# Moving two DMA destinations in SBUF from 128 bytes past a multiple of 256 to a multiple of 4096

## The chip, the cores and the metric

One core of one Trainium2 chip. The metric is the device time of one execution in microseconds (us). A comparison uses runs of both kernels taken in the same rounds on the same chip. Single runs are marked as such below.

Some terms. HBM is the memory outside the core, SBUF the core's own memory, used here in 128 partitions. In this kernel's trace TensorE runs the matrix multiplications, VectorE copies and reductions, ScalarE the activations. A packet is the trace's record of a piece of work on one of the 16 DMA engines: a load of 8 MB gives 128 packets of 64 KB, as many as there are partitions. By a descriptor the text means the order for one such piece, so it takes a packet for a descriptor. "PV" in the prediction is the multiplication of the probabilities with the values.

## The reference

Two attention layers decode one token each, and their outputs stand side by side. Layer A has 32 heads and reads all 32768 keys of each; layer B has 32 query heads on 8 key heads and reads the last 4096 keys. Everything is bfloat16.

```python
def _A_ref(x, k_cache, v_cache, wq, wo):            # H = 32, Sk = 32768, Dh = 128
    q = (x @ wq).reshape(B, Sq, H, Dh)...
    scores = einsum("bhqd,bhkd->bhqk", q, k_cache) * Dh ** -0.5
    o = einsum("bhqk,bhkd->bhqd", softmax(scores), v_cache)
    return o... @ wo
# B: the same over k_cache[:, :, Sk - 4096:, :] with 8 key heads
return concatenate([a, b], axis=-1)
```

Layer A's caches alone are 32 heads x 2 x 8 MB. Nothing is used twice, so the kernel is a stream from HBM with enough arithmetic beside it to keep up.

## The kernel before

All buffers are allocated one after another in each partition of SBUF. `kbuf` holds three parts of 32 KB a partition, `vbuf` two. A head of A needs two parts of each: 64 KB in each of 128 partitions, 8 MB. The head's keys are transposed on TensorE into `kt`, multiplied with the query, and the probabilities are multiplied with the values straight from `vbuf`.

```python
    def alloc(self):
        nc = self.nc
        sb = nc.alloc_sbuf_tensor
        self.kbuf = sb("kbuf", [128, 3 * HALF * DH], BF16)      # HALF = DH = 128
        self.vbuf = sb("vbuf", [128, 2 * HALF * DH], BF16)
        self.kt = [sb(f"kt{i}", [128, 1024], BF16) for i in range(NKT)]
        self.psb = sb("psb", [128, 512], BF16)
        # ... the small buffers ...

    def load(self, dst, src, sem, *deps):
        self.op("sp", lambda e: e.dma_start(dst, src).then_inc(sem, 16), *deps)

    # ...
    def kv_src(self, which, name, g):
        d = self.X[name]
        src = d[which][0, g * d["kvg"]:(g + 1) * d["kvg"], d["key0"]:d["key0"] + d["NKEYS"], :]
        return src.rearrange("s (p j) d -> p s (j d)", p=128)

    # ...
    def load_k(self, g, parts):
        w = HALF * DH
        src = self.kv_src("k", "A", g)[:, 0, :]
        lo = min(self.k_thirds(g))
        free = [self.free["k"][t] for t in self.k_thirds(g)]
        if parts == 1:                                          # heads 1 to 30
            self.load(self.kbuf[:, w * lo:w * lo + 2 * w], src, self.mark("k", 0), *free)
            sem = self.mark("k", 1)
            self.op("sp", lambda e: e.sem_inc(sem, 16), self.free["k"][0] if g == 1 else None)
        else:
            for i, t in enumerate(self.k_thirds(g)):
                self.load(self.kbuf[:, w * t:w * t + w], src[:, w * (t - lo):w * (t - lo) + w], self.mark("k", i), *free)

    def load_v(self, g):
        self.load(self.vbuf[:, :], self.kv_src("v", "A", g)[:, 0, :], self.mark("v", 0), *self.free["v"])
    # ... B's loads and the weights go into the same two buffers, in pieces of 3 to 32 KB a partition ...
```

The compiled program places `kbuf` at byte 16512 of each partition and `vbuf` at 114816; both are 128 past a multiple of 256.

## Time and profile before

| | before |
|---|---|
| time, median of 3 runs | 1327.09 us (1326.9 to 1327.21) |
| DMA queue 1, share of 16 engines' span | 99.7% |
| DMA rate, 100 to 1200 us | 433 to 434 GB/s |
| TensorE / VectorE busy | 73% / 57% |
| TensorE's wait for a head's keys | 157.2 us in 31 waits |

Two lines of the page's table of DMA queues. They give packets, MB, and the time that the packets took as a share of the span of 16 engines:

```profile
q1 hardware_dynamic: 13190, 570.44, 99.7%
...
HBM read 570.43 MB, written 0.00 MB: 431 GB/s over the span
```

Busy time by stretches of the span. After the stretch and its length come the engines' busy times, then the granted clock, the DMA share and GB/s as the last three numbers:

```profile
100.00:400.00 300.00, 217.86 (x2952) 151.61 (x2952) 163.90 (x289) 12.68 (x40) 0.00 (x0) 0.82 1.00 433
400.00:800.00 400.00, 300.08 (x4160) 211.24 (x4158) 234.82 (x411) 15.86 (x50) 0.00 (x0) 0.84 1.00 433
800.00:1200.00 400.00, 294.81 (x4057) 204.69 (x4054) 226.63 (x400) 17.44 (x55) 0.00 (x0) 0.84 1.00 434
```

A DMA share of 1.00 in all three, while no engine is busy more than 76% of a stretch, is what a kernel bound by its transfers looks like. The instruction groups say the same from the other side: count, busy time and mean of one, then the idle time before them and who ended it.

```profile
L563 DVE COPY kt<-psT 128x1024 bf16<-128x1024 bf16 x1056 | 654.8, 684 | 239.6 <-PE psT L559 237.6
L559 PE MATMUL psT<-ident,kbuf 128*128 128x128 bf16 x8448 | 578.2, 234 | 171.7 <-DMA kbuf<-in_A_k_cache_dram 157.2
...
L662 PE MATMUL psACC<-vbuf,ptsb 128*4 128x512 bf16 (+1 forms) x2112 | 186.2, 529 | 22.8 <-ACT ptsb L637 22.0
```

TensorE waits for a key landing once a head, 5 us on average. The DMA queue for its part waits for buffers to come free. From the list of waits, first the queue's own, then TensorE's (total us, times, longest):

```profile
SPq L326 <- PE psACC L662: 632.2, 32, 21.0
SPq L326 <- PE psS L582: 612.5, 35, 26.5
```

```profile
PE psT L559 <- DMA kbuf<-in_A_k_cache_dram: 157.2, 31, 10.0
...
PE psT L559 <- DMA kbuf<-in_B_k_cache_dram: 11.0, 2, 6.2
```

And from the table of DMA issues, where the last number is the median time from issue to landing in us:

```profile
vbuf<-in_A_v_cache_dram SPq DMA_DIRECT2D x32, 26.6
...
kbuf<-in_A_k_cache_dram SPq DMA_DIRECT2D x30, 27.8
```

The queue's long waits look alarming and are not: 8 MB at 434 GB/s take 19.3 us, and a load lands 26.6 to 27.8 us after its issue, so each is issued while the one ahead still runs and the engines do not run dry (DMA share 1.00 from 100 to 1200 us). A shorter transfer therefore shortens the kernel, by up to those 5 us a head. The unit to look at is the single packet. The trace has each packet of the queue with its size and duration; sorted by size, this is a count that the page does not print:

```
packets of queue 1, kernel before: bytes, count, median ns, the most frequent durations (ns, count)
65536 x7936  2422   2422 x2448, 2418 x1374, 2426 x1275, 2419 x1091, 2420 x673, 2421 x350, ...
16384 x256    615    615 x60,    611 x57,    619 x36, ...
 8192 x2176   312    309 x798,   314 x359,   312 x275, 321 x248, ...
 4096 x128    161    159 x52,    161 x16, ...
```

Between 16 and 64 KB the medians rise by 1807 ns for 49152 bytes, which is 1.176 ns for 32 bytes. The rest, about 12.6 ns at both sizes (10.8 at 8 KB, 10.4 at 4 KB), does not go with the bytes.

### The profile page before, as it was taken

The page shows a single profiled execution, that of the slowest core. Times are in us where ns is not written, and L with a number is a line of the kernel's source. Part 1 is how long each engine was busy: PE and PEld are TensorE (multiplying, and loading weights), DVE is VectorE, ACT ScalarE, POOL GpSimd, SP SyncE. Part 2 cuts the span into 40 slices and gives each one's busy share as a digit, 9 for nine tenths or more (in the row PEclk, how much of TensorE's full clock was granted, in tenths as well). Part 3 has the DMA queues.
Part 4 walks back from the last instruction along what each step waited for, and adds up shares of the span by engine and source line. Part 5 has one row for each costly group of instructions (what it writes and reads, how often), then busy time and mean ns, then how long its engine had stood idle before and what let it go on. Part 6 is the DMA issues. An engine that isn't in the chain of part 4 may idle for free. (4 is left out here: it accounts for less than half of the span.)

```text
span 1324.9 us, 28805 instructions
## 1 busy us (share of the span) xinstructions
PE 966.8 (73%) x13243; PEld 673.9 (51%) x13243; DVE 751.2 (57%) x1341; ACT 54.8 (4%) x167; POOL 2.6 (0%) x22
## 2 busy tenths in 40 slices
PE   4675778777677878767787876778786677868786
PEld 3453446555444655544465544446554445655453
DVE  3563556664555666455566645556664556665563
ACT  0000000000000000000000000000000000000000
POOL 0000000000000000000000000000000000000000
PEclk8886788887878888787888878788887879887898
DMA  9999999999999999999999999999999999999998
GB/s 403 430 434 430 441 429 427 441 435 427 436 433 437 427 437 435 427 439 431 427 441 433 435 429 433 437 427 439 434 427 439 431 431 437 431 437 429 433 437 350
DMA packets 13489, 570.60 MB, mean 431 GB/s; under 512 B 1827, under 2 KB 1830, under 8 KB 2214
## 3 DMA queue, kind: packets, MB, share of 16 engines
q1 hardware_dynamic: 13190, 570.44, 99.7%
q8 instruction: 8, 0.13, 0.0%
q10 hardware_dynamic: 288, 0.00, 0.0%
q14 instruction: 3, 0.02, 0.0%
HBM read 570.43 MB, written 0.00 MB: 431 GB/s over the span
## 5 line engine op out<-in xcount | busy, mean ns | idle before, releaser
L563 DVE COPY kt<-psT 128x1024 bf16<-128x1024 bf16 x1056 | 654.8, 684 | 239.6 <-PE psT L559 237.6
L559 PE MATMUL psT<-ident,kbuf 128*128 128x128 bf16 x8448 | 578.2, 234 | 171.7 <-DMA kbuf<-in_A_k_cache_dram 157.2
L559 PEld LDWEIGHTS psT<-ident,kbuf 128*128 128x128 bf16 x8448 | 538.5, 106 | 263.9 <-DMA kbuf<-in_A_k_cache_dram 165.3
L662 PE MATMUL psACC<-vbuf,ptsb 128*4 128x512 bf16 (+1 forms) x2112 | 186.2, 529 | 22.8 <-ACT ptsb L637 22.0
L582 PE MATMUL psS<-kt,qw 128*32 128x512 bf16 x2048 | 157.8, 385 | 15.0 <-DVE kt L563 15.0
L676 DVE TENSOR_SCALAR oc_A<-psACC,hot_A 128x128 f32<-128x128 f32 x32 | 11.2, 351 | 250.8 <-PE psG L689 250.8
L662 PEld LDWEIGHTS psACC<-vbuf,ptsb 128*4 128x4 bf16 (+1 forms) x2112 | 60.3, 111 | 139.1 <-issue 91.4
L610 ACT ACTIVATE psb<-psS,nb_A 128x512 bf16<-128x512 f32 x32 | 22.0, 687 | 1168.4 <-DVE nb_A L609 1168.4
L582 PEld LDWEIGHTS psS<-kt,qw 128*32 128x32 bf16 x2048 | 34.1, 95 | 57.6 <-DVE kt L563 30.7
L689 PE MATMUL psG<-oc_A,hw 128*32 128x128 f32 (+1 forms) x128 | 19.3, 227 | 52.3 <-DVE oc_A L678 52.3
L689 PEld LDWEIGHTS psG<-oc_A,hw 128*32 128x32 f32 x128 | 11.4, 109 | 62.4 <-DVE oc_A L678 55.1
L634 PE MATMUL psPT<-ident,psb 128*128 128x128 bf16 x136 | 18.1, 275 | 34.0 <-ACT psb L610 34.0
L678 DVE SCALAR_TENSOR_TENSOR oc_A<-psACC,hot_A,oc_A 128x128 f32<-128x128 f32 x96 | 33.7, 351 | 3.4
L599 DVE TENSOR_REDUCE tr_in<-psS 128x1 f32<-128x512 f32 x34 | 23.5, 692 | 17.3 <-PE psS L582 17.3
L634 PEld LDWEIGHTS psPT<-ident,psb 128*128 128x128 bf16 x136 | 10.2, 118 | 37.0 <-ACT psb L610 36.7
L603 PE MATMUL psACC<-rows,tr_in 128*1 128x64 f32 x64 | 8.7, 217 | 25.6 <-DVE tr_in L599 25.6
L637 ACT ACTIVATE ptsb<-psPT 128x512 bf16<-128x512 bf16 x34 | 20.3, 597 | 31.1 <-PE psPT L634 31.1
L603 PEld LDWEIGHTS psACC<-rows,tr_in 128*1 128x1 f32 x64 | 2.7, 81 | 35.3 <-DVE tr_in L599 35.3
L607 PE MATMUL psACC<-mr_A,nscale 1*128 1x1 f32 x64 | 12.1, 256 | 9.7 <-DVE mr_A L606 9.7
L607 PEld LDWEIGHTS psACC<-mr_A,nscale 1*128 1x128 f32 x64 | 9.4, 183 | 15.7 <-DVE mr_A L606 15.7
L609 DVE COPY nb_A<-psACC 128x1 f32<-128x1 f32 x32 | 5.0, 157 | 15.1 <-PE psACC L607 15.1
L606 DVE TENSOR_REDUCE mr_A<-psACC 1x1 f32<-1x64 f32 x32 | 6.8, 212 | 11.7 <-PE psACC L603 11.7
(81 smaller groups left out, 72.0 us busy)
## 6 DMA issues: line engine op xcount, KB each, us to landing
kbuf<-in_A_k_cache_dram SPq DMA_DIRECT2D x4, 4096.0 KB, 22.9
kbuf<-in_B_k_cache_dram SPq DMA_DIRECT2D x2, 4096.0 KB, 31.8
vbuf<-in_B_v_cache_dram SPq DMA_DIRECT2D x2, 4096.0 KB, 25.6
vbuf<-in_B_wq_dram SPq DMA_DIRECT2D x1, 4096.0 KB, 12.4
vbuf<-in_A_wq_dram SPq DMA_DIRECT2D x1, 4096.0 KB, 31.9
kbuf<-in_B_wo_dram SPq DMA_DIRECT2D x2, 2048.0 KB, 33.7
kbuf<-in_A_wo_dram SPq DMA_DIRECT2D x1, 1408.0 KB, 28.1
kbuf<-in_A_wo_dram SPq DMA_DIRECT2D x1, 1024.0 KB, 30.2
```

The source lines that it names most:

```text
L559: inst = e.transpose(T[:, 128 * k:128 * k + 128], src[:, DH * k:DH * k + DH], self.ident[:, :])
L563: self.copies.append(self.op("dve", lambda v: v.tensor_copy(KT[:, :], T[:, :]), o, to="pe"))
L582: inst = e.matmul(self.S[32 * c:32 * c + 32, :], lhsT=win, rhs=self.kt[(bb + c // 2) % NKT][:, 512 * (c % 2):512 * (c % 2) + 512], start=b ...
L599: o = dve(lambda v: v.reduce_max(tr["in"][:, 0:1], self.S[:, :], axis=AXX), self.sdone, self.k_pool, to="pe" if name == "A" else None)
L603: o = self.op("pe", lambda e: e.matmul(self.ACC[0:1, 0:64], lhsT=tr["in"][:, 0:1], rhs=self.rows64[:, :], start=True, stop=True, skip_grou ...
L607: o = self.op("pe", lambda e: e.matmul(self.ACC[:, 64:65], lhsT=self.nscale[:, :], rhs=t["mr"][0:1, :], start=True, stop=True, skip_group_ ...
L610: self.sread = self.op("act", lambda s: s.activation(out=self.psb[:, :], in_=self.S[:, :], func=ACTF.Exp, bias=t["nb"][:, k:k + 1], scale= ...
L634: inst = e.transpose(PT[:, 128 * jj:128 * jj + 128], self.psb[:, 128 * jj:128 * jj + 128], self.ident[:, :])
L637: self.ptread = self.op("act", lambda s: s.activation(out=self.ptsb[:, :], in_=PT[:, 0:512], func=ACTF.Copy), self.psread, to="pe")
L662: inst = e.matmul(acc[32 * c:32 * c + rows, 0:512], lhsT=lhsT, rhs=rhs, start=begin, stop=end, tile_position=(0, 32 * c), skip_group_check ...
L678: o = self.op("dve", lambda v, src=src, hot=hot: v.scalar_tensor_tensor(out=oc, in0=src, scalar=hot, in1=oc, op0=ALU.mult, op1=ALU.add), p ...
L689: return self.op("pe", lambda e: e.matmul(self.G[0:32, c0 + c:c0 + c2], lhsT=win, rhs=t["oc"][g % len(t["oc"])][:, c:c2], start=False, sto ...
```

## The change

The two buffers that all large transfers write are to start at multiples of 4096 bytes of a partition. Each DMA descriptor then starts on a round address. Nothing else is touched.

```diff
-        self.kbuf = sb("kbuf", [128, 3 * HALF * DH], BF16)
-        self.vbuf = sb("vbuf", [128, 2 * HALF * DH], BF16)
+        self.kbuf = sb("kbuf", [128, 3 * HALF * DH], BF16, align_bytes=4096)
+        self.vbuf = sb("vbuf", [128, 2 * HALF * DH], BF16, align_bytes=4096)
```

`kbuf` moves to byte 20480, `vbuf` to 118784, and all buffers behind them move by the same 3968 bytes. The instructions of every engine are the same in number and order.

## The prediction

> **What bounds the kernel.** The transfers into the key and value buffers. The busy-time table by stretches gives a DMA share of 1.00 and 433 to 434 GB/s from 100 to 1200 us; the queue table gives queue 1 99.7% of 16 engines' span, about 1321 of 1324.9 us. TensorE is busy 73%, VectorE 57%. In the list of waits TensorE waits for a key landing once a head, 5 us of about 38.7 on average, so compute has slack. The DMA queue waits for buffers (632 us on PV, 612 us on the scores) but does not starve: an 8 MB load takes 26.6 to 27.8 us from issue to landing, its bytes about 19.3 us, so one is always waiting behind the one that runs.
>
> **What a packet costs.** The trace's packets of queue 1, by size (median): 64 KB 2422 ns (x7936), 32 KB 1218 (x768), 16 KB 615 (x256), 8 KB 312 (x2176), 4 KB 161. From 16 to 64 KB that is 1.176 ns per 32 bytes, 27.2 GB/s an engine[...]. What remains is about 12.6 ns a packet. 11648/16 = 728 large packets an engine make it 9.2 us.
>
> **What the change does.** kbuf moves from byte 16512 to 20480 of each partition, vbuf and everything behind it by the same 3968 bytes. Instructions stay the same. Every DMA destination in the two buffers begins a multiple of 1 KB from the buffer's start, so today each starts 128 bytes past a multiple of 256, afterwards none. [...] Estimate: 4 x 1.176 = 4.7 ns a packet, x 728 = 3.4 us. At most the whole constant goes, 9 us. [...]
>
> **How much is critical.** All of it: the queue is never empty, so the time is the packets' time over 16 plus about 5 us of head and tail. The engines' means should not change (transposes 234 ns, copies 684, PV matmuls 529).
>
> **Predicted time:** 1323.7 us, 8 in 10 between 1318.5 and 1327.3. Faster by over 2%: 0.02; within 2%: 0.97; slower by over 2%: 0.01.
>
> **What would show it.** 64 KB packets at about 2417 ns in place of 2422, 8 KB ones shorter by the same 5 ns: the constant falls from 12.6 to about 8 ns, the slope stays at 1.176. The wait for keys shrinks by 0.1 us a head, too little to see.
>
> **What would make it wrong.** [...] A gain over 2% would need a slope under 1.176 ns[...].

The sum came to 3.4 us off the 1327.1 us of before, 1323.7 us. Its 4.7 ns are the estimate: that the 128 bytes between the multiple of 256 below and the start of a packet cost as much as 128 bytes moved, so 4 times the 1.176 ns that the trace gives for 32 bytes, once a packet. That they do was an assumption that no run had shown, and so was that the slope of 1.176 ns cannot get lower.

## The result, and the profile after

| | before | after |
|---|---|---|
| time, median of 6 runs | 1327.12 us (1326.84 to 1327.25) | 1324.14 us (1323.8 to 1326.55) |
| ratio to before, 95% interval | | 0.9981 (0.9968 to 0.9994) |
| span of the profiled run | 1324.9 us | 1322.0 us |
| packet time of queue 1, summed, / 16 | 1321.5 us | 1318.9 us |
| 64 KB packets, mean without outliers | 2421.71 ns | 2418.00 ns |

A ratio here is the mean time of one kernel's fast runs over that of the other's of the same rounds, so it is not quite the ratio of the medians. One of the six runs after took 1326.55 us, at a granted clock of 0.831 against 0.836 to 0.838 of the others; it widens the interval. "Without outliers" leaves out packets more than 40 ns over the shortest, 6 of 7936 after.

The same views of the kernel after: queue table, stretches, groups, wait for keys, landings.

```profile
q1 hardware_dynamic: 13190, 570.44, 99.8%
...
HBM read 570.43 MB, written 0.00 MB: 432 GB/s over the span
```

```profile
100.00:400.00 300.00, 216.42 (x2952) 151.26 (x2956) 163.54 (x288) 11.90 (x38) 0.00 (x0) 0.82 1.00 434
400.00:800.00 400.00, 302.74 (x4176) 213.09 (x4176) 236.82 (x413) 15.86 (x50) 0.00 (x0) 0.83 1.00 435
800.00:1200.00 400.00, 293.96 (x4036) 205.51 (x4036) 225.83 (x397) 17.43 (x55) 0.00 (x0) 0.84 1.00 434
```

```profile
L563 DVE COPY kt<-psT 128x1024 bf16<-128x1024 bf16 x1056 | 654.9, 684 | 237.5 <-PE psT L559 235.7
L559 PE MATMUL psT<-ident,kbuf 128*128 128x128 bf16 x8448 | 579.1, 234 | 168.5 <-DMA kbuf<-in_A_k_cache_dram 154.6
...
L662 PE MATMUL psACC<-vbuf,ptsb 128*4 128x512 bf16 (+1 forms) x2112 | 185.2, 527 | 23.2 <-ACT ptsb L637 21.3
```

```profile
PE psT L559 <- DMA kbuf<-in_A_k_cache_dram: 154.6, 31, 11.1
```

```profile
vbuf<-in_A_v_cache_dram SPq DMA_DIRECT2D x32, 26.3
...
kbuf<-in_A_k_cache_dram SPq DMA_DIRECT2D x30, 27.6
```

The last two are TensorE's wait for keys and the landings: 2.6 us less waiting in 31 heads, and loads that land 0.2 to 0.3 us sooner. The packet counts are as before, and the transposes and copies take what they took (234 and 684 ns). The stretches show 434 to 435 GB/s for 433 to 434, at the edge of what they can show. The packets show it plainly:

```
packets of queue 1, kernel after: bytes, count, median ns, the most frequent durations (ns, count)
65536 x7936  2418   2418 x7929, one of 2424, six from 2659 to 2968
16384 x256    611    611 x256
 8192 x2176   309    309 x2169, ...
 4096 x128    159    159 x128
```

Not only is the mean lower: the spread is gone. The slope is the same (1807 ns for 49152 bytes). A line through the medians of all sizes of this profile rises by 1.1765 ns for 32 bytes, and what is left over that is 8.2 ns, 7 times as much, for every size from 3 to 64 KB (7.8 to 8.6, with durations in whole ns). The summed packet time fell by 2.66 us, the span by 2.9.

### The profile page after: what moved, and what is told of

It reads as the page before. It is cut to its first block, busy times and chain, and to the rows that moved or that the text cites. A ratio compares the mean times of both kernels' runs of the same rounds, so it can differ in the third digit from the quotient of the medians.

```text
span 1322.0 us, 28805 instructions
## 1 busy us (share of the span) xinstructions
PE 966.2 (73%) x13243; PEld 674.9 (51%) x13243; DVE 751.3 (57%) x1341; ACT 54.8 (4%) x167; POOL 2.6 (0%) x22
## 5 line engine op out<-in xcount | busy, mean ns | idle before, releaser
L501 PE MATMUL psACC<-vbuf,x_B 128*2 128x512 bf16 x32 | 3.6, 627 | 13.5 <-DMA x_B<-in_B_x_dram 13.5
```

## The experiments

The theory going in (A): a packet whose destination does not start at a multiple of 256 bytes pays a constant. Its rivals: the 4096 of the change matters (B); the buffers behind moved too, and the compute engines gain by it (C); the gain is fixed or goes with the bytes (D). Within A it was open how the constant depends on the distance, and whether the HBM side pays as well. In the table below a 64 KB packet's mean is without outliers; a mean from 7936 packets of one profile tells apart what the time of one run cannot (three kernels with the same 128 gave 2421.71, 2421.72 and 2421.74).

| run | `kbuf`/`vbuf` start, past a multiple of 256 | 64 KB packets, ns | time, us | before in the same rounds, us |
|---|---|---|---|---|
| before | 128 | 2421.71 | 1327.12 | |
| after | 0 (4096) | 2418.00 | 1324.14 | 1327.12 |
| off256 | 0 (256 past 4096) | 2418.00 | 1324.21 (4 runs) | 1327.17 |
| off32 | 32 | 2422.63 | 1327.80 (1 run) | 1327.17 |
| off64 | 64 | 2421.80 | 1327.53 (1 run) | 1327.09 |
| off224 | 224 | 2422.63 | 1328.06 (1 run) | 1327.17 |
| rest_moved | 128 | 2421.74 | 1327.23 (4 runs) | 1327.17 |
| src128_dst0 | 0, reads off by 128 | 2418.00 | 1323.82 (1 run) | 1327.41 |
| src224_dst0 | 0, reads off by 224 | 2418.00 | 1324.52 (1 run) | 1327.09 |
| src128_dst128 | 128, reads off by 128 | 2421.72 | 1327.43 (1 run) | 1327.41 |
| k_only | keys 0, values 128 | 2418.52 | 1325.14 (4 runs) | 1327.09 |

### Which multiple counts: off256

```diff
+        sb("padk", [128, 64], BF16)
         self.kbuf = sb("kbuf", [128, 3 * HALF * DH], BF16)
```

The pad of 128 bytes puts `kbuf` at 16640 and `vbuf` at 114944, both 256 past a multiple of 4096.

> Key and value buffers at a multiple of 256 bytes that is no multiple of 4096 (byte 16640). Theory A (what counts is the start against 256 bytes): 64 KB packets at 2418 ns, all alike, as in the kernel after; time 1324 us. Rival B (the 4096 of the change matters[...]): packets as before, 2422 ns on average with a spread from 2418 to 2433, time 1327 us.

Measured: 7929 of 7936 packets at 2418 ns, and 1324.21 us (ratio 0.9976, interval 0.9959 to 0.9993). B falls: a multiple of 256 gives all that the 4096 gave. Whether a smaller multiple would do is answered by the next runs.

### How the price goes with the distance: off32, off224, off64

The same line with pads of 80, 48 and 96 elements.

> Buffers 32 bytes past a multiple of 256. Theory A1 [...] 1.2 ns a packet, so a mean of about 2419.5 ns for 64 KB against 2418.3 after and 2422.1 before; time about 1325 us. Rival A2 [...]: 2422 ns as before, 1327 us.

> Buffers 224 bytes past a multiple of 256. Theory A1: [...] 8.2 ns a packet, so about 2426.5 ns for 64 KB and 1330 us, slower than before. Rival A2: 2422 ns as before, 1327 us.

> Buffers 64 bytes past a multiple of 256. If the price is for the start off 256 and does not go with the distance (off32 and off224: 4.6 ns, 128: 3.7 ns): 64 KB packets at 2421.7 to 2422.7 ns, 1327 to 1328 us. If only starts off a multiple of 64, or less, paid: impossible beside the 128 of the kernel before. If it goes with the distance from the nearer multiple of 256 after all: 3 ns or less.

A1 is the prediction's estimate carried over: the bytes between the multiple of 256 below and the start cost as much as bytes moved, 1.176 ns for 32, so 1.2 ns at 32 and 8.2 at 224. A2 is a price that does not go with the distance.

Measured: 4.63 ns over the aligned packet at 32 bytes and the same 4.63 at 224; 3.80 at 64; 3.71 at 128. By A1, 32 and 224 would be 1.2 and 8.2 ns. A1 falls, and with it the assumption behind the prediction's 4.7 ns. The rival A2 comes within 1 ns of all four. It is not the whole story: the 0.8 to 0.9 ns more at 32 and 224, both 32 bytes from a boundary, is far above what separates repeats (0.03 ns), and no run here explains it. The counts of 32 and 224 are almost the same number for number:

```
64 KB packets: ns, count
off32    2421 x4440, 2428 x1734, 2420 x749, 2419 x501, 2426 x489, ...
off224   2421 x4440, 2428 x1734, 2420 x749, 2419 x501, 2426 x488, ...
off64    2420 x4020, 2427 x1463, 2419 x742, 2418 x444, 2425 x411, ...
```

A 64 KB write that starts 32 past a boundary begins with 224 bytes up to the next one and ends with 32; at 224 it is the other way round. The two cost the same (2422.63 ns), so which of the two part pieces comes first does not matter. In all these runs a packet also spans 257 blocks of 256 bytes in place of 256. Whether the price belongs to that additional block is not shown.

### The buffers behind: rest_moved

```diff
         self.vbuf = sb("vbuf", [128, 2 * HALF * DH], BF16)
+        sb("pade", [128, 64], BF16)
         self.kt = [sb(f"kt{i}", [128, 1024], BF16) for i in range(NKT)]
```

> Key and value buffers stay where before has them; everything behind them moves by 128 bytes to a multiple of 256, as in the change. Theory A: nothing changes, 64 KB packets at 2422 ns, 1327 us. Rival C (the gain comes from the compute engines reading and writing kt, psb and the constants at better addresses): 1324 us and packets at 2418 ns, or at least shorter transposes and copies than 234 and 684 ns.

Measured: 1327.23 us (ratio 0.9999, interval 0.9982 to 1.0016), packets at 2421.74 ns with the old spread. Transposes and copies took 235 and 683 ns, as the first two of these groups of its page show. C falls for the buffers behind.

```profile
L564 DVE COPY kt<-psT 128x1024 bf16<-128x1024 bf16 x1056 | 656.8, 683 | 243.9 <-PE psT L560 242.3
L560 PE MATMUL psT<-ident,kbuf 128*128 128x128 bf16 x8448 | 584.7, 235 | 171.7 <-DMA kbuf<-in_A_k_cache_dram 156.5
...
L663 PE MATMUL psACC<-vbuf,ptsb 128*4 128x512 bf16 (+1 forms) x2112 | 182.9, 521 | 22.8 <-ACT ptsb L638 22.0
```

TensorE also reads `kbuf` and `vbuf`, which this run leaves in place. For those the groups of before and after answer: 234 ns for the transposes in both, 529 and 527 ns for the multiplication with the values, whose mean was 521 in rest_moved with `vbuf` unmoved.

### The read side: src128_dst0, src224_dst0, src128_dst128

```diff
+        if name == "A":
+            n = d["SK"] * DH
+            at = n * g + (64 if g < NQH - 1 else 64 - 128)      # 112 for src224_dst0
+            flat = d[which].rearrange("b h s d -> (b h s d)")
+            return flat[at:at + n].rearrange("(s p x) -> p s x", s=1, p=128)
         src = d[which][0, g * d["kvg"]:(g + 1) * d["kvg"], ...]
```

These read every key and value of A from a place shifted in HBM, so the result is wrong (relative error 0.28). The first two build on the kernel after, the third on the kernel before. Theory E takes the prediction's estimate over to the reads: 4 x 1.176 = 4.7 ns a packet at 128 bytes, and 7 x 1.176 = 8.2 ns at 224, which the second expectation calls "that".

> Wrong result on purpose: buffers aligned, but A's keys and values are read 128 bytes off a multiple of 256 in HBM. Theory E (reads pay too[...]): about 2422 to 2423 ns for 64 KB packets, 1327 us. Rival F (only the write side's start counts): 2418 ns, 1324 us.

> Wrong result on purpose: buffers aligned, A's reads 224 bytes past a multiple of 256[...]. If reads pay that: 2426 ns, 1328 us or more. If, as with 128, reads pay nothing that shows: 2418 ns, 1324 us.

> Wrong result on purpose: buffers as before and the reads shifted by the same 128 bytes, so both sides are off by the same. Theory G (the price is for read and write lying differently against the 256 byte grid): 2418 ns, 1324 us. Theory E (each side pays its own): 2426 ns, 1330 us. Theory F (the write alone): as before, 2422 ns, 1327 us.

Measured: with aligned buffers 7929 of 7936 packets take 2418 ns at both read shifts; with the buffers of before, 2421.72 ns. Shifting the reads changes nothing, alone or together with the writes. (Whatever the tensors' own addresses, at least two of the three read positions 0, 128 and 224 lie off a multiple of 256.) E and G fall, F holds: only the destination's start shows in the time here. Whether the reads pay nothing, or something that does not show in a packet's time, these runs cannot tell.

### More packets: split_off128 and split_aligned

```diff
-        if parts == 1:
-            self.load(self.kbuf[:, w * lo:w * lo + 2 * w], src, self.mark("k", 0), *free)
-            ...
+        c = 2 * w // 16
+        for x in range(0, 2 * w, c):
+            self.load(self.kbuf[:, w * lo + x:w * lo + x + c], src[:, x:x + c], self.mark("k", 0), *free)
+        sem = self.mark("k", 1)
+        self.op("sp", lambda e: e.sem_inc(sem, 16), self.free["k"][1 - g] if g < 2 else None)
 # load_v likewise; once on the kernel before, once on the kernel after
```

> Each 8 MB load of A as 16 loads of 512 KB (4 KB a partition), buffers where before has them. Theory A (a constant per packet that starts off a multiple of 256): 131072 packets of 4 KB in place of 8192 of 64 KB, at about 162 ns each as the 128 in the kernel before; 8192 an engine x 162 = 1327 us, with semaphore packets and the rest about 1420 us. To be read against split_aligned.

> The same 16 loads, buffers at multiples of 4096. Theory A: 159 ns a packet, so 3 ns x 8192 an engine = 25 us less than split_off128, about 1397 us: the gain of the change grows with the number of packets, from 3 us to 25. Rival D (the gain is a fixed one, or goes with the bytes): 3 us less.

The "semaphore packets" are the 4 byte packets of queue 1: 1403 in the profile before, 9 ns each (median).

Measured: 1405.77 us against 1371.93, so 33.8 us or 2.4% between two kernels that differ in the alignment alone. The 131200 packets of 4 KB take 163.10 ns on average where the buffers are off and 159.00 (131162 of them exactly 159) where they are aligned. 4.10 ns x 8192 packets an engine is 33.6 us, so the time agrees with the packets. D falls: the gain grew elevenfold with the number of packets. My 25 us were too low because I took 162 ns from the 128 such packets of the kernel before.

Both totals came out lower than expected (1420 and 1397), and the page says why. The queue line, the same in both runs, and the stretches, first of split_off128, then of split_aligned:

```profile
q1 hardware_dynamic: 151142, 570.50, 101.6%
```

```profile
400.00:800.00 400.00, 277.40 (x3868) 196.09 (x3864) 216.84 (x382) 14.27 (x45) 0.00 (x0) 0.83 1.03 410
800.00:1200.00 400.00, 276.94 (x3793) 193.29 (x3794) 212.67 (x374) 15.86 (x50) 0.00 (x0) 0.80 1.03 410
```

```profile
400.00:800.00 400.00, 289.19 (x3960) 202.93 (x3960) 223.23 (x390) 15.86 (x50) 0.00 (x0) 0.82 1.03 420
800.00:1200.00 400.00, 288.08 (x3960) 204.17 (x3960) 223.69 (x390) 15.86 (x50) 0.00 (x0) 0.82 1.03 420
```

A DMA share of 1.03, and 101.6% of the span in the queue line, mean that packets of these two runs overlap a little in time, so their durations add up to more than the span; the sum of packet times, which my expectation used, is an upper bound for them. The rate is what to compare: 410 against 420 GB/s.

### One buffer alone: k_only

```diff
+        sb("padk", [128, 64], BF16)
         self.kbuf = sb("kbuf", [128, 3 * HALF * DH], BF16)
+        sb("padv", [128, 64], BF16)
         self.vbuf = sb("vbuf", [128, 2 * HALF * DH], BF16)
```

> Key buffer at a multiple of 256, value buffer 128 bytes past one. The price is per packet and by its own start: half of the 64 KB packets exactly 2418 ns, half as before (mean 2421.7), together a mean of 2419.9, and half the gain: 1325.6 us. If one buffer's alignment made the whole gain: 1324 or 1327 us.

Measured: 1325.14 us (ratio 0.9986, interval 0.9969 to 1.0002, which does not exclude no change). The packets decide: 6871 of 7936 take exactly 2418 ns where I expected half, and the mean is 2418.52 where I expected 2419.9. The summed packet time over 16 is 1319.4 us, so 2.1 of the 2.7 us are there with one buffer of two aligned. The price does not simply add up by packet. The loads alternate, values and keys, 128 packets each. I put the 64 KB packets in order of their start, cut them into loads, and averaged over the loads of the steady part (the 9th to the 60th of 62) what each packet took over the 2418 ns, by sixteenths of a load. In this part of both runs the 16 engines end a load within 2.24 us of each other, less than one packet, so the cut does not mix loads:

```
mean ns over the aligned packet, by sixteenth of a load, in order of start
before, values  2.9 3.9 1.7 3.4 3.5 1.1 3.6 4.3 5.1 3.4 3.7 5.1 4.8 3.4 3.8 5.1   mean 3.7
before, keys    3.6 2.8 3.0 1.3 3.1 4.5 4.6 3.0 4.3 4.8 5.0 3.3 3.8 5.0 4.8 3.4   mean 3.8
k_only, values  0.0 0.0 0.0 0.0 0.0 0.0 0.0 0.0 0.0 0.0 0.4 0.1 2.5 0.4 3.3 4.5   mean 0.7
k_only, keys    3.0 2.4 1.0 0.4 0.0 0.0 0.0 0.0 0.0 0.0 0.0 0.0 0.0 0.0 0.0 0.0   mean 0.4
```

In k_only the misaligned values cost nothing for the first ten sixteenths of a load; then the price appears, runs over into the first packets of the aligned keys, and is gone for the rest of them. That reads as a slack that the misaligned load uses up and the aligned one restores. An estimate of it: a values load of before pays 8 packets x 3.7 = 30 ns an engine, of which 8 x (0.7 + 0.4) = 9 show in k_only, so some 20 ns are absorbed per pair of loads. This is one reading of one run; what holds the slack is not shown.

### Start, end, or count: edges

```diff
 ...
-            self.load(self.kbuf[:, w * lo:w * lo + 2 * w], src, self.mark("k", 0), *free)
+        for x, y in ((64, 2 * w), (0, 64)):
+            self.load(self.kbuf[:, w * lo + x:w * lo + y], src[:, x:y], self.mark("k", 0), *free)
 ...
-        self.load(self.vbuf[:, :], self.kv_src("v", "A", g)[:, 0, :], self.mark("v", 0), *self.free["v"])
+        src, n = self.kv_src("v", "A", g)[:, 0, :], 2 * HALF * DH
+        for x, y in ((0, n - 192), (n - 192, n)):
+            self.load(self.vbuf[:, x:y], src[:, x:y], self.mark("v", 0), *self.free["v"])
```

It builds on the kernel after; lengths are in elements of 2 bytes.

> Buffers at multiples of 4096. A's keys come as a 65408 byte piece that starts 128 bytes past a multiple of 256 and ends on one, and the 128 bytes ahead of it; A's values as a 65152 byte piece that starts on a multiple of 256 and ends 128 bytes past one, and the 384 bytes behind it. Without any extra they would take 65408/32 + 7 = 2051 cycles of 1.1765 ns = 2412.9 ns, and 65152/32 + 7 = 2043 = 2403.5 ns. H1 [...]: neither is over, both spreads vanish[...]. H2 (the price is for the start): keys at about 2416.6 ns with a spread, values at 2403.5 without. H3 [...]: both about 2 to 4 ns over. Time well over 1327 us, as there are twice the packets.

The sizes' times are an estimate from the packets of the kernel after: what the expectation calls a cycle is the slope of 1.1765 ns for 32 bytes, and 7 of these are the 8.2 ns left over. The three hypotheses, in terms of addresses: H1, a packet pays when it touches one more block of 256 bytes than its size needs, which neither large piece does; H2, it pays when it starts off a multiple of 256; H3, it pays when either end is off one.

Measured: 1335.57 us (one run). 3509 of 4096 key pieces take exactly 2413 ns, yet the mean is 2414.06, 1.1 ns over; 3880 of 4096 value pieces take 2404, mean 2404.27 (both without outliers). So none of the three came out as written. H3 is the furthest off, as pieces that only end off a boundary pay next to nothing (their 384 byte neighbours start off one, which muddies the run further; 4085 of these 4096 take 22 ns, and 12 x 1.1765 + 8.2 = 22.3 ns is the estimate for a packet of 384 bytes without extra, as 4 x 1.1765 + 8.2 = 12.9 ns is for the keys' 128 byte pieces, which take 13; so their misaligned start shows no price of its own, though the slack of k_only could hide one). H1 (no price, no spread) does not hold for the keys, and H2's 3.7 ns are not reached. But after k_only a mix of loads that are off and loads that are not says little: k_only paid 1.1 ns per misaligned packet too (0.7 + 0.4), and there H2's condition certainly held. The keys' price also grew with time, from nothing in most early heads to about 1.7 ns late. Whether a misaligned start alone costs, or only the additional block of 256 bytes that a packet touches, stays open. A run with all large pieces starting off a boundary and none touching an additional block would tell.

No version beat the kernel after: off256 equals it within the noise.

## Why the prediction was right or wrong

- **What bounds the kernel: right.** The summed packet time fell by 2.66 us, the span by 2.9 and the median by 3.0. What the packets lose the kernel loses.
- **No large gain: right.** The slope of 1.176 ns per 32 bytes was the same before and after, so the alignment changed nothing that goes with the bytes, and the rate rose only from 433 to 434 GB/s to 434 to 435. That the slope could not get lower was the assumption; a limit on it is not shown.
- **A constant per packet, on the destination's side: right.** split_off128 and split_aligned show that it multiplies with the packets (33.8 us), src128_dst0 and src224_dst0 show no cost for the start of the reads (2418.00 ns a packet in both).
- **Its size: a little high.** "Estimate: 4 x 1.176 = 4.7 ns a packet, x 728 = 3.4 us." Measured 3.71 ns for a 64 KB packet and 2.66 us in all. The constant fell from about 12.6 ns (by medians) to 8.2, as predicted ("to about 8"). 8 KB packets became shorter by 4.0 ns in the mean (313.01 to 309.00, without outliers), where the prediction had 5.
- **Its mechanism: wrong.** The step that failed is the 4 in "4 x 1.176": the assumption that the 128 bytes below the start cost as much as bytes moved. The price is 4.63 ns at 32 bytes and at 224 alike. That the number came near was luck, because 128 bytes happen to be 4 times 32; at 224 bytes the same reasoning would have said 8.2 ns. In its place the runs show a price of 3.71 to 4.63 ns at each of the four starts off a multiple of 256 (32, 64, 128 and 224), which shrinks when the loads between are aligned (k_only). What makes this price stays open.
- **The alternative that only reads pay: wrong the other way round.** In these runs a price shows for the start of the writes alone.
- **The engines' means: right.** 234, 684 and 527 ns; and rest_moved, where `kt`, `psb` and the constants move alone, gains nothing.

## What to carry to other kernels

Where the DMA queue is busy from end to end, sort its packets by size and split their time into a slope and a constant: a slope that a change does not touch (here 1.176 ns for 32 bytes before and after) leaves nothing to gain there, and the constant is what each descriptor costs. Start the destinations of large transfers at a multiple of 256 bytes of a partition, as these runs favour; here that was worth about 4 ns a descriptor and engine, 0.2% with 64 KB descriptors and 2.4% with 4 KB ones. Even aligned, cutting 64 KB into 4 KB cost 48 us here (1324.14 to 1371.93), far more than the misalignment ever did, so make the descriptors long first.
